# PSUM banks 4 to 7 as buffers of their own, keys loaded whole, values without regrouping, a re-planned order and zero matmuls, in a fused attention and feed-forward kernel on one core

## The chip, the core and the metric

The kernel runs on one core of a Trainium2 chip. The metric is the device time of one execution in microseconds (us), the median over runs. The profile is one execution recorded by the hardware profiler; its span runs from the first to the last instruction.

## The reference, cut to what matters

```python
batch, n_heads, seq, head_dim = (8, 8, 576, 64); n_pack = 32
def sm_attn(qq, kk, vv):                       # softmax(qq kk^T / 8) vv, per batch and head
    ...
p_packed = sm_attn(p, k, v)                    # 32 packed rows attend to 576 keys
out = sm_attn(q, p_packed, p_packed)           # 576 queries attend to the 32 packed rows
x = out.transpose(0, 2, 1, 3).reshape(4608, 512)
h = x @ w_in                                   # 512 -> 2048
g = np.maximum(h, 0.0) ** 2
return g @ w_out                               # 2048 -> 512
```

Inputs and output are float32; the kernel computes in bfloat16 with float32 accumulation.

## The kernel before, in words

**Work of one batch.** A batch has 8 heads, held as two groups ("qd") of four heads. Its steps carry short names, which the planner uses:

- Lk, Lq, Lv: loads of keys, queries and values, issued by POOL, which also turns them into bfloat16. Each key tile comes in two DMAs (L361, one for each half of a row's positions), each query tile in one (L357), the values of a batch in two (L366).
- Tk, Tq: 32x32 block transposes of the keys (L398) and queries (L393) on VectorE.
- G: a copy (L320 on VectorE) that regroups the loaded values v_b into v_g, so that two heads' 128 columns lie side by side.
- S1: scores of the packed rows, six matmuls (L409, L412); then the row maximum on VectorE (L416), the exponential on ACT (L420), the normalisation on VectorE (L426, L427). E: transposes of the result on TensorE (L433) and a copy out (tile e).
- PV: the packed values, ten matmuls for each qd, of 128 weight columns by 64 (L447). XT: eight small casts into the block-diagonal pq_bd and two casts into ppT.
- M: w_in times the packed values, four chunks of 512 columns, each chunk eight matmuls of 64x32 tiles (L474), then copies out to M. Because the second attention has only 32 packed rows, w_in is applied to these rows and not to all 576 queries.
- S2: scores of the queries (L495, L502); then maximum and subtraction (L514, L519), exponential on ACT (L525), sum, reciprocal and product on VectorE (L531, L532, L537). N: transposes of the result (L544, L547) and a copy out to a.
- F1: 16 steps of four matmuls (L560, M times a), each followed by a relu (L572 on ACT, L574 on VectorE) and a square (L582 on VectorE, L580 on ACT) into gT.
- F2: 36 output tiles of 128 tokens, each 16 matmuls of 512 columns (L590) that add up in one PSUM bank, then a copy to o_sb (L318 on ACT, L320 on VectorE) and four DMAs to the output. A batch is 4.5 such tiles.

**Order.** All engines work through their instructions in the order in which the program lists them. That order is made by a planner in the kernel (class Plan): it simulates the engines with assumed durations per step, takes at each moment the step with the best priority among the streams of steps (loads, transposes, first attention, M, second attention, F1, F2), and the instructions are then emitted in the order of the planned starts. TABLE holds an offset to each step's priority and a bias against ACT. HOP is the time assumed between a step's end and the start of what needs it. The loads stand in one stream: keys, values and queries of batch 0, w_in in 8 DMAs, half of w_out, batch 1 with the rest of w_out, then batches 2 to 7.

**PSUM.** Eight banks lie in four buffers of two banks each (`ps`). Banks 0 and 1, and 2 and 3, take S1, S2 and F1 (and, for some steps, F2); 4 and 5 take E, PV, N and the rest of S2; 6 and 7 take F2 tiles by turns. M takes banks 4 and 5 together with 0 and 1 or 2 and 3. What an instruction has to wait for is worked out by the framework from the buffers that it and earlier instructions touch.

**Slots.** 12 buffers hold key and query tiles, 4 hold values. POOL's loads take turns on eight DMA semaphores: a load waits until the load eight before it has landed.

`keep_clock` (a loop of matmuls of the zero tile with itself into the bank that is used next) exists before, but its count, `plan.fill`, stays 0 because `plan.warm` is 0.

Of the kernel before, what the change touches and what calls it, by code (L numbers as in the profile page):

```python
# [8 lines left out]
ACT = mybir.ActivationFunctionType  # L9
# [5 lines left out]
P = 128  # L15
# [9 lines left out]
HOP = 0.2  # L25
# [23 lines left out]
class Plan:  # L49
# [13 lines left out]
    def forward(self):  # L63
# [36 lines left out]
        while heap:  # L100
# [4 lines left out]
            while True:  # L105
# [40 lines left out]
                if e != "-":  # L146
                    busy[e] = f
                out.append(pc)
# [41 lines left out]
    def aim(self):  # L190
        for steps in self.streams:
            for st in steps:
                st.prio = self.prio.get(st.key, self.level(st))
                st.late = st.prio - (50.0 if st.key[:2] == "F2" else 0.25)
                st.lean = self.lean.get(st.key, 0.0)
# [6 lines left out]
    def run(self):  # L202
# [5 lines left out]
        for p in sorted(out, key=lambda p: p.start):  # L208
            e, us, fn = p.alts[p.alt]
            if e == "PE":  # L210
                self.fill = self.fills(p.start - free.get(e, 0.0), p.start)
# [15 lines left out]
TABLE = {'o': {'F1.1': -111.4, 'E.7': -15.38, 'F2.12': 29.55, 'F2.10': 62.36, 'PV.7': -8.82, 'Tk.5': -56.4, 'G.4':  # L227
    36.96, 'F2.32': 85.58, 'P.2': 78.86, 'G.2': 14.69, 'Tk.2': 14.82, 'Tq.2': 38.02, 'S1.2': -11.08, 'E.2': -36.13,
    'PV.2': 40.19, 'XT.2': 5.83, 'M.2': -3.06, 'S2.2': -26.61, 'C.2': -103.21, 'N.2': 47.99, 'F1.2': -28.89, 'C.5':
    -77.4, 'PV.4': -100.26, 'M.7': 3.35, 'G.3': -17.95, 'XT.0': 38.77, 'XT.1': 61.95, 'XT.3': -9.46, 'XT.4': -19.74,  # L230
    'XT.5': 39.77, 'XT.6': -76.62, 'XT.7': 28.4, 'F2.1': 28.92, 'P.0': 2.97, 'F2.24': 39.64, 'C.1': -16.13, 'C.3':
    -60.08, 'C.4': -34.32, 'C.6': -66.73, 'C.7': -8.09, 'X.0': 8.45, 'X.1': -10.2, 'I': -23.25, 'Tq.0': 5.27, 'Tq.3':
    67.76, 'G.5': 39.3, 'Tq.5': 26.97, 'S1.5': 3.18, 'E.5': -27.04, 'PV.5': 9.13, 'M.5': 25.95, 'S2.5': -32.33, 'N.5':
    60.11, 'F1.5': 20.76, 'F2.22': 41.33, 'E.4': -50.69, 'F2.4': 70.11, 'F1.0': 50.99, 'F1.3': 9.7, 'F1.4': -10.94,
    'F1.6': -33.13, 'F1.7': 61.34, 'S1.7': -26.63, 'Tk.3': 10.86, 'G.0': 18.04, 'Tk.0': 0.11, 'S1.0': -5.5, 'E.0':
    -43.01, 'PV.0': 24.59, 'M.0': 6.9, 'S2.0': -14.32, 'N.0': 3.07, 'F2.34': 79.86, 'F2.15': 128.64, 'Tk.4': -9.27,
    'Tq.4': -47.79, 'S1.4': -16.59, 'M.4': 25.83, 'S2.4': -4.33, 'N.4': -24.9, 'G.1': 11.86, 'G.6': 14.66, 'G.7':
# [632 lines left out]
```

## Time and profile before

| | |
|---|---|
| time, median of 3 runs | 310.99 us (308.6 to 311.1) |
| the profiled execution | 310.96 us, span 309.2 us |
| TensorE busy | 251.5 us (81%), 1920 matmuls |
| VectorE busy | 202.3 us (65%) |
| ACT busy | 163.8 us (53%) |
| POOL busy | 59.7 us (19%) |
| loads through POOL's queue | 18.60 MB in 33552 packets |
| chain that ended last | TensorE 65%, DMA 12%, ACT 9%, VectorE 8% |

How to read the lines below: a line of the timeline has the start (us from the span's start), the time taken, the engine (PE is TensorE, PEld its weight loads, DVE VectorE, SP the queue that issues the output DMAs), the line of the kernel, the operation, output<-input with shapes, a count, and in brackets how long the engine sat idle before it and what ended that. Ends of matmuls are modelled and include the passage through the pipeline. A line of the waits reads: who <- for whom: us in total, times, longest. The rows of the 40 slices give busy tenths of each engine; the DMA row is the busy share of the 16 DMA engines.

### The profile page before, as it was taken

What the parts mean: (1) busy time and instruction counts of PE and PEld (TensorE: products, weight loads), DVE (VectorE), ACT (ScalarE), POOL (GpSimd) and SP (SyncE); (2) the same over time, 40 slices, a digit from 0 to 9 for tenths busy, and PEclk for the clock granted to TensorE, in tenths of its full rate; (3) what the DMA queues carried; (4) which work ended last, traced back from release to release, by engine and by line L of the source; (5) the groups of instructions that cost most, each with busy time, mean ns of one, the idle gap of its engine ahead of it and who ended that gap; (6) DMA issues with size and microseconds to landing.
All of it is one profiled execution on the core that took longest, in us unless ns stands there. A gap on an engine that the chain in (4) does not pass through costs nothing.

```text
span 309.2 us, 5088 instructions
## 1 busy us (share of the span) xinstructions
PE 251.5 (81%) x1920; PEld 143.4 (46%) x1920; DVE 202.3 (65%) x370; ACT 163.8 (53%) x298; POOL 59.7 (19%) x91
## 2 busy tenths in 40 slices
PE   0244459769899899999999998899999898998883
PEld 0132326335555365555635564465655552465331
DVE  3667457888998856877997589765788456364000
ACT  3134346956734376666564766668876404274110
POOL 7559566530514010060000000000000000000000
PEclk9999999989999999999999999999999999999999
DMA  5999999998499861139321111111110121211222
GB/s 48 190 205 204 187 202 187 191 181 146 46 167 189 189 102 45 37 42 183 75 60 44 34 37 34 37 35 44 38 33 24 51 53 34 70 35 27 58 54 68
DMA packets 41016, 28.50 MB, mean 92 GB/s; under 512 B 17952, under 2 KB 34336, under 8 KB 40992
## 3 DMA queue, kind: packets, MB, share of 16 engines
q0 software_dynamic: 33552, 18.60, 41.5%
q1 hardware_dynamic: 6912, 9.45, 11.2%
q8 instruction: 15, 0.25, 0.4%
q10 hardware_dynamic: 528, 0.13, 0.2%
q14 instruction: 9, 0.07, 0.1%
HBM read 37.22 MB, written 9.44 MB: 151 GB/s over the span
## 4 chain that ended last, share of the span: by engine, by line
PE 65%; DMA 12%; ACT 9%; DVE 8%; issue 3%; POOL 1%; ACTq 0%; DVEq 0%; POOLq 0%
PE ps L590 38%; PE ps L560 17%; ACT o_sb L318 4%; DMA w_in_b<-in_moe_w_in_dram 3%; DMA q_b<-in_q_dram 3%; DMA w_out_b<-in_moe_w_out_dram 3%; DMA k_b<-in_k_dram 2%; ACT r L572 2%; PE ps L474 2%; PE ps L495 2%; PE ps L409 2%; DVE o_sb L320 1%; PE ps L544 1%; PE ps L433 1%; PE ps L447 1%
## 5 line engine op out<-in xcount | busy, mean ns | idle before, releaser
L590 PE MATMUL ps<-w_out_b,gT 128*128 128x512 bf16 x576 | 148.2, 380 | 15.0 <-ACT o_sb L318 11.8
L572 ACT ACTIVATE r<-ps 128x576 bf16<-128x576 f32 (+1 forms) x132 | 77.7, 611 | 41.7 <-PE ps L560 36.6
L560 PE MATMUL ps<-a,M 128*128 128x288 bf16 x512 | 83.4, 293 | 4.7 <-ACT r L572 1.7
L590 PEld LDWEIGHTS <-gT 128*128 128x128 bf16 x576 | 54.0, 98 | 62.8 <-issue 17.0
L560 PEld LDWEIGHTS <-M 128*128 128x128 bf16 x512 | 50.1, 100 | 39.7 <-issue 15.2
L582 DVE TENSOR_TENSOR gT<-r 128x576 bf16<-128x576 bf16 x121 | 51.6, 448 | 21.7 <-ACT r L572 20.7
L318 ACT COPY o_sb<-ps 128x512 f32<-128x512 f32 x27 | 15.8, 586 | 42.3 <-PE ps L590 38.3
L361 POOL DMA_DIRECT2D k_b<-in_k_dram x32 | 22.3, 703 | 38.8 <-DVE qT L393 22.7
L318 ACT CAST M<-ps 128x1024 bf16<-128x1024 f32 (+1 forms) x28 | 24.2, 896 | 10.4 <-PE ps L474 10.4
L398 DVE STREAM_TRANSPOSE kT<-k_b 128x1152 bf16<-128x1152 bf16 x16 | 21.5, 1361 | 9.5 <-DMA k_b<-in_k_dram 9.5
L409 PE MATMUL ps<-kT,pT_bd 128*128 128x256 bf16 x64 | 11.3, 307 | 14.8 <-DVE kT L398 14.6
L393 DVE STREAM_TRANSPOSE qT<-q_b 128x1152 bf16<-128x1152 bf16 x16 | 21.7, 1366 | 1.9 <-DMA q_b<-in_q_dram 1.9
L420 ACT ACTIVATE e1x<-ps,n 128x576 bf16<-128x576 f32 x16 | 11.9, 744 | 11.1 <-DVE n L416 8.3
L514 DVE TENSOR_REDUCE m<-ps 128x4 f32<-128x128 f32 (+2 forms) x17 | 11.8, 716 | 7.2 <-PE ps L495 4.3
L416 DVE TENSOR_REDUCE n<-ps 128x1 f32<-128x576 f32 x16 | 11.9, 745 | 5.7 <-PE ps L412 5.7
L474 PE MATMUL ps<-w_in_b,ppT 64*32 64x512 bf16 x256 | 11.2, 402 | 5.1 <-DVE d L519 2.1
L409 PEld LDWEIGHTS <-pT_bd 128*128 128x128 bf16 x64 | 6.3, 106 | 18.0 <-issue 9.6
L357 POOL DMA_DIRECT2D q_b<-in_q_dram x16 | 8.9, 560 | 25.4 <-DVE qT L393 18.7
L433 PE MATMUL ps<-ident,e1n 128*128 128x128 bf16 x80 | 8.2, 241 | 6.9 <-DVE e1n L427 6.6
L318 ACT COPY a<-ps 128x576 bf16<-128x576 bf16 x12 | 7.4, 640 | 11.7 <-PE ps L547 8.4
L525 ACT ACTIVATE e<-d 128x1152 bf16<-128x1152 f32 (+2 forms) x10 | 9.7, 969 | 6.4 <-DVE d L519 6.3
L531 DVE TENSOR_REDUCE t<-e 128x36 f32<-128x1152 bf16 (+2 forms) x10 | 11.0, 1103 | 2.3 <-ACT e L525 2.2
(54 smaller groups left out, 207.0 us busy)
## 6 DMA issues: line engine op xcount, KB each, us to landing
out_dram<-o_sb SPq DMA_DIRECT2D x144, 64.0 KB, 1.7
k_b<-in_k_dram POOLq DMA_DIRECT2D x32, 144.0 KB, 7.9
q_b<-in_q_dram POOLq DMA_DIRECT2D x16, 288.0 KB, 9.3
v_b<-in_v_dram POOLq DMA_DIRECT2D x8, 320.0 KB, 9.5
v_b<-in_v_dram POOLq DMA_DIRECT2D x8, 256.0 KB, 8.8
w_in_b<-in_moe_w_in_dram POOLq DMA_DIRECT2D x8, 256.0 KB, 10.2
w_out_b<-in_moe_w_out_dram POOLq DMA_DIRECT2D x8, 256.0 KB, 10.0
p_b<-in_p_dram POOLq DMA_DIRECT2D x1, 192.0 KB, 10.4
```

Source lines behind the costliest of these rows:

```text
L318: nc.scalar.copy(dst, src)
L361: nc.gpsimd.dma_start(t[:, j2 * VX * D:(j2 + 1) * VX * D], src[j2])
L393: nc.vector.transpose(self.qT[:, qd].rearrange("p dh (j a) -> p j dh a", a=32), self.t.q[qd][:].rearrange("p (j dh dl) -> p j dh dl", dh=2 ...
L398: nc.vector.transpose(kT[:, qd].rearrange("p dh (j a) -> p j dh a", a=32), self.t.k[qd][:].rearrange("p (j dh dl) -> p j dh dl", dh=2, dl=32))
L409: nc.tensor.matmul(main[:, i], lhsT=w[dh], rhs=kv[dh][:, i * GM:(i + 1) * GM], start=(dh == 0), stop=(dh == 1))
L416: nc.vector.tensor_reduce(self.n1[:, qd:qd + 1], self.ps1[qd], axis=AX.X, op=ALU.max, negate=True)
L420: nc.scalar.activation(e1x[:, qd], self.ps1[qd], ACT.Exp, bias=self.n1[:, qd:qd + 1], accum_out=self.d1[:, qd:qd + 1])
L474: nc.tensor.matmul(pair(u, j)[o:o + 32, qd, :], lhsT=self.ppT[64 * e:64 * e + 64, qd, pr, :], rhs=w_in_b[64 * e:64 * e + 64, qd * 2 + pr, ...
L560: nc.tensor.matmul(ps[:, c], lhsT=a.M[:, qd, fb * FB:(fb + 1) * FB], rhs=a.a2[:, qd, c * HALF:(c + 1) * HALF], start=(qd == 0), stop=(qd = ...
L572: nc.scalar.activation(dst, src, ACT.Relu)
L582: eng.tensor_tensor(out=Att.cols(gT[:, fb, o:o + S]), in0=r, in1=r, op=ALU.mult)
L590: nc.tensor.matmul(po[t], lhsT=gT[:, fb, n0:n0 + P], rhs=w_out_b[:, fb, :], start=(fb == 0), stop=(fb == NFB - 1))
```

## The change

- **PSUM.** Banks 0 to 3 stay as two buffers of two; banks 4 to 7 become four buffers of one bank each (`pb4` to `pb7`). M's second chunk of a pair is copied out of its two single banks by halves.
- **Keys.** One DMA loads a whole key tile, like a query tile. The positions then stand in another order along a row, and S1's matmuls write their scores with a stride of two columns, which restores the order that the values have.
- **Values.** v_g and its copies are gone; PV reads v_b as loaded. A weight tile is now one head's 64 columns, so PV has 20 matmuls of 64 weight columns by 32 for each qd instead of 10 of 128 by 64. The two heads of a pair land in the two halves of the partitions, so that ppT is one cast instead of two.
- **Slots.** 16 buffers for keys and queries, 5 for values.
- **Order.** A new TABLE, a new set of assumed durations, HOP 0.07 instead of 0.2 with 0.13 added after TensorE's steps, loads limited to eight under way in the plan and served in line. F2 tiles form two streams, the even and the odd ones. In the built order both N of batch 0 stand ahead of S1 of batch 1 (before: one of them after it); ahead of N of batch 1 stand 64 matmuls of F1 and 32 of F2 (before: 56 and 16). After the last F1 matmul 63 matmuls of F2 remain (before: 82).
- **Zero matmuls.** `plan.warm = 70.0`: where the plan has a gap of more than 0.45 us on TensorE within its first 70 us, matmuls of the zero tile (128x128 by 256 columns) are put in, one for each 0.115 us of the gap less 0.2. There are 160, in groups of 44, 6, 14, 4, 14, 11, 19, 11, 11, 4, 2, 13 and 7 in this order.

The numbers that TABLE holds are left out.

```diff
 INF = float("inf")
-HOP = 0.2
+HOP = 0.07
+LATE = {"PE": 0.13}
...
                 pc.start, pc.end, pc.alt = t, f, a
                 if e != "-":
                     busy[e] = f
+                f += LATE.get(e, 0.0)
                 out.append(pc)
...
             for st in steps:
                 st.prio = self.prio.get(st.key, self.level(st))
                 st.late = st.prio - (50.0 if st.key[:2] == "F2" else 0.25)
+                if st.key[0] == "L":
+                    st.late = -200.0 + 1e-3 * steps.index(st)
                 st.lean = self.lean.get(st.key, 0.0)
...
-            if e == "PE":
-                self.fill = self.fills(p.start - free.get(e, 0.0), p.start)
+            self.fill = self.fills(p.start - free.get(e, 0.0), p.start) if e == "PE" else 0
...
-    NKQ, NV = 12, 4
+    NKQ, NV = 16, 5
...
-        v_g = [consts.tile([P, GM + 1, H * D], BF16, name=f"v_g{i}") for i in range(2)]
         gT = consts.tile([P, NFB, 2 * S], BF16, name="gT")
-        ps = [psum.tile([P, 2, 512], F32, name=f"ps{i}") for i in range(4)]
+        ps = [psum.tile([P, 2, 512], F32, name=f"ps{i}") for i in range(2)]
+        ps += [psum.tile([P, 512], F32, name=f"pb{i}") for i in range(4, 8)]
...
         def keep_clock(t):
             for _ in range(plan.fill):
                 nc.tensor.matmul(t, lhsT=zero[:, :P], rhs=zero, start=True, stop=True)
             plan.fill = 0
 
+        def half(n):
+            return ps[n // 2][:, n % 2, :] if n < 4 else ps[n - 2][:]
+
         def bank(u, j=0):
-            t = ps[u[j] // 2][:, u[j] % 2, :]
+            t = half(u[j])
             keep_clock(t[:, :2 * P])
             return t
 
         def pair(u, j=0):
-            assert u[j] % 2 == 0 and u[j + 1] == u[j] + 1
+            assert u[j] in (0, 2) and u[j + 1] == u[j] + 1
             keep_clock(ps[u[j] // 2][:, 0, :2 * P])
             return ps[u[j] // 2]
...
-                self.v_raw, self.v = v_b[b % NV], v_g[b % 2]
+                self.v = v_b[b % NV]
 
             def dma_kq(self, name, qd):
                 t = getattr(self, name)[qd] = qkv.tile([P, JT * D], BF16, name=name + "_b", tag="kqb")
-                if name == "q":
-                    nc.gpsimd.dma_start(t, q[self.b, qd * QH:(qd + 1) * QH].rearrange("h (a j) d -> (h a) (j d)", j=JT))
-                else:
-                    src = k[self.b, qd * QH:(qd + 1) * QH].rearrange("h (j2 a x) d -> j2 h a (x d)", j2=2, x=VX)
-                    for j2 in range(2):
-                        nc.gpsimd.dma_start(t[:, j2 * VX * D:(j2 + 1) * VX * D], src[j2])
+                src = {"k": k, "q": q}[name]
+                nc.gpsimd.dma_start(t, src[self.b, qd * QH:(qd + 1) * QH].rearrange("h (a j) d -> (h a) (j d)", j=JT))
 
             def dma_v(self, i):
                 n = GM + i
                 src = v[self.b].rearrange("h (ap x) d -> ap h (x d)", x=VX)
-                nc.gpsimd.dma_start(self.v_raw[64 * i:64 * i + 64, :, :n * D], src[:, :, i * GM * D:(i * GM + n) * D])
-
-            def group(self, h0, h1, eng):
-                cast(eng, self.v[:, :, h0 * D:h1 * D].rearrange("p g (h d) -> p h g d", d=D),
-                     self.v_raw[:, h0:h1].rearrange("p h (g d) -> p h g d", d=D))
+                nc.gpsimd.dma_start(self.v[64 * i:64 * i + 64, :, :n * D], src[:, :, i * GM * D:(i * GM + n) * D])
...
                 ps = self.ps1[qd] = pair(u).rearrange("p c n -> p (c n)")[:, :S]
                 kv = [kT[:, qd, dh].rearrange("p (j2 x a) -> p x j2 a", j2=2, a=32) for dh in range(2)]
                 w = [pT_bd[:, self.b, qd, dh] for dh in range(2)]
-                main = ps[:, :GM * P].rearrange("p (g i n) -> p i g n", i=2, n=64)
+                main = ps[:, :GM * P].rearrange("p (g i a j2) -> p i g j2 a", i=2, a=32, j2=2)
+                rest = ps[:, GM * P:].rearrange("p (a j2) -> p j2 a", j2=2)
                 for i in range(2):
                     for dh in range(2):
                         nc.tensor.matmul(main[:, i], lhsT=w[dh], rhs=kv[dh][:, i * GM:(i + 1) * GM],
                                          start=(dh == 0), stop=(dh == 1))
                 for dh in range(2):
-                    nc.tensor.matmul(ps[:, GM * P:], lhsT=w[dh], rhs=kv[dh][:, 2 * GM], start=(dh == 0), stop=(dh == 1))
+                    nc.tensor.matmul(rest, lhsT=w[dh], rhs=kv[dh][:, 2 * GM], start=(dh == 0), stop=(dh == 1))
...
             def pv(self, qd, u):
                 if qd == 0:
-                    self.ps_pp = bank(u)
-                ps = self.ps_pp
+                    self.ps_pp = bank(u)[:, :P]
                 for pr in range(2):
-                    h0 = qd * QH + 2 * pr
-                    c0 = qd * P + pr * 64
+                    c0 = (2 * qd + pr) * NP
                     for g in range(GM + 1):
-                        nc.tensor.matmul(ps[:, c0:c0 + 64], lhsT=self.t.v[:, g, h0 * D:(h0 + 2) * D],
-                                         rhs=self.e1[:, qd, g, pr * 64:pr * 64 + 64], start=(g == 0), stop=(g == GM))
-
-            def extract(self, e, eng):
+                        for e in range(2):
+                            h = 2 * pr + e
+                            nc.tensor.matmul(self.ps_pp[64 * e:64 * e + 64, c0:c0 + NP],
+                                             lhsT=self.t.v[:, qd * QH + h, g * D:(g + 1) * D],
+                                             rhs=self.e1[:, qd, g, h * NP:(h + 1) * NP], start=(g == 0), stop=(g == GM))
+
+            def extract(self, eng):
                 self.tile_of("ppT", small, [P, NQD, 2, NP], BF16)
-                cast(eng, self.ppT[64 * e:64 * e + 64].rearrange("p qd pr i -> p (qd pr) i"),
-                     self.ps_pp[64 * e:64 * e + 64, :2 * P].rearrange("p (n i2 i) -> p n i2 i", i2=2, i=NP)[:, :, e])
+                cast(eng, self.ppT[:].rearrange("p qd pr i -> p (qd pr i)"), self.ps_pp)
...
             def m(self, c, u, j=0):
                 self.tile_of("M", mpool, [P, NQD, DFF], BF16)
+                keep_clock(half(u[j])[:, :2 * P])
                 for h in range(QH):
                     for qd in range(NQD):
                         pr, e = divmod(h, 2)
                         o = 32 * (h ^ qd)
-                        nc.tensor.matmul(pair(u, j)[o:o + 32, qd, :], lhsT=self.ppT[64 * e:64 * e + 64, qd, pr, :],
+                        nc.tensor.matmul(half(u[j + qd])[o:o + 32], lhsT=self.ppT[64 * e:64 * e + 64, qd, pr, :],
                                          rhs=w_in_b[64 * e:64 * e + 64, qd * 2 + pr, c * WCH:(c + 1) * WCH],
                                          start=True, stop=True)
-                self.psm[c] = pair(u, j)
+                self.psm[c] = u[j:j + 2]
 
             def m_out(self, c, eng):
-                cast(eng, self.M[:, :, c * WCH:(c + 1) * WCH], self.psm[c])
+                cast(eng, self.M[:, :, c * WCH:(c + 1) * WCH], ps[self.psm[c][0] // 2])
 
             def m_half(self, c, qd, eng):
-                cast(eng, self.M[:, qd, c * WCH:(c + 1) * WCH], self.psm[c][:, qd])
+                cast(eng, self.M[:, qd, c * WCH:(c + 1) * WCH], half(self.psm[c][qd]))
...
-        plan = Plan({"kqb": NKQ, "vb": NV, "r": 4, "osb": 3}, 8)
+        plan = Plan({"kqb": NKQ, "vb": NV, "r": 4, "osb": 3, "dq": 8}, 8)
...
-        def load_step(name, us, fn, slot=(), issue=0.62):
-            return Step(name, [[[("POOL", issue, fn)]], [[("DMA", us, lambda: None)]]], (), slot, (), lag=1.8)
+        def load_step(name, us, fn, slot=[], issue=0.56):
+            return Step(name, [[[("POOL", issue, fn)]], [[("DMA", us, lambda: None)]]], (), slot + [("dq", 1)], [("dq", 1, None)], lag=LAG)
...
         def pv_steps(b):
             nm = f"PV.{b}.0"
-            return [Step(nm, [[[("PE", 0.45, lambda: T[b].pv(0, U[nm]))]]],
-                         [f"E.{b}.0", f"G.{b}.0"], banks=AB),
-                    Step(f"PV.{b}.1", [[[("PE", 0.45, lambda: T[b].pv(1, U[nm]))]]],
-                         [f"E.{b}.1", f"G.{b}.1"]),
+            return [Step(nm, [[[("PE", 0.29, lambda: T[b].pv(0, U[nm]))]]],
+                         [f"E.{b}.0", f"Lv.{b}.0", f"Lv.{b}.1", "I2" if b else "I"], banks=AB),
+                    Step(f"PV.{b}.1", [[[("PE", 0.29, lambda: T[b].pv(1, U[nm]))]]],
...
                                        ("ACT", 0.82, lambda x=x: T[b].pq_block(x, A))] for x in range(2)]
-                                     + [[("DVE", 0.23, lambda e=e: T[b].extract(e, V)),
-                                         ("ACT", 0.24, lambda e=e: T[b].extract(e, A))] for e in range(2)]],
+                                     + [[("DVE", 0.27, lambda: T[b].extract(V)),
+                                         ("ACT", 0.28, lambda: T[b].extract(A))]]],
...
@@ -698,12 +684,14 @@
                 def mm(c=c, nm=nm):
                     T[b].m(c, U[nm], 0)
                     T[b].m(c + 1, U[nm], 2)
-                res.append(Step(nm, [[[("PE", 0.66, mm)]],
-                                     [[("ACT", 1.02, lambda x=x: T[b].m_out(x, A)),
-                                       ("DVE", 1.22, lambda x=x: T[b].m_out(x, V))] for x in (c, c + 1)]],
-                                [f"XT.{b}/1.{i}" for i in (2, 3)] + [f"LWI.{x}.{i}" for x in (c, c + 1) for i in range(2)]
+                res.append(Step(nm, [[[("PE", 0.56, mm)]],
+                                     [[("ACT", 1.02, lambda c=c: T[b].m_out(c, A)),
+                                       ("DVE", 1.22, lambda c=c: T[b].m_out(c, V))]]
+                                     + [[("ACT", 0.6, lambda c=c, x=x: T[b].m_half(c + 1, x, A)),
+                                         ("DVE", 0.7, lambda c=c, x=x: T[b].m_half(c + 1, x, V))] for x in QDS]],
+                                [f"XT.{b}/1.2"] + [f"LWI.{x}.{i}" for x in (c, c + 1) for i in range(2)]
                                 + ([f"F1.{b - 2}.{NFB - 1}"] if b > 1 else []),
-                                banks=[(4, 5) + x for x in HB], free=[(1, None)]))
+                                banks=[x + (4, 5) for x in HB], free=[(1, None)]))
...
+        LAG = 2.4
...
-        plan.base.update(DVE=3.0, POOL=0.8, ACT=0.8, SP=0.3, DMA=2.5, PE=3.6)
+        plan.base.update(DVE=2.4, POOL=1.2, ACT=2.1, SP=0.3, DMA=3.0, PE=3.0)
...
-        plan.stream(sum([g_steps(b) for b in range(B)], []))
...
         plan.stream(sum([f1_steps(b) for b in range(B)], []))
-        plan.stream(f2_steps(0))
-        plan.stream(f2_steps(1))
-        x, y = f2_steps(2, "F2.2.0", 0), f2_steps(3, "F2.2.0", 1)
-        plan.stream([z for i in range(NFB) for z in (x[i], y[i])])
-        plan.stream(sum([f2_steps(t) for t in range(4, NT)], []))
+        plan.stream(sum([f2_steps(t) for t in range(0, NT, 2)], []))
+        plan.stream(sum([f2_steps(t) for t in range(1, NT, 2)], []))
         plan.use(TABLE)
+        plan.warm = 70.0
```

## The prediction

> **What bounds the kernel now.** I read the page first (spans, the 40 slices, the chain), then the table by stage, then TensorE's waits after the start-up, then three stretches of the timeline.
>
> ```profile
> span 309.2 us, 5088 instructions
> PE 251.5 (81%) x1920; PEld 143.4 (46%) x1920; DVE 202.3 (65%) x370; ACT 163.8 (53%) x298; POOL 59.7 (19%) x91
> PE   0244459769899899999999998899999898998883
> DMA  5999999998499861139321111111110121211222
> ```
>
> ```profile
> 0.00:68.06 68.06, 33.32 (x281) 20.80 (x282) 44.07 (x84) 32.74 (x70) 43.36 (x66) 0.99 1.19 178
> 68.06:304.20 236.14, 218.19 (x1641) 122.58 (x1640) 158.23 (x286) 130.49 (x227) 16.32 (x25) 1.00 0.35 68
> ```
>
> The stage rows give the time in PE, PEld, DVE, ACT and POOL, then the granted clock, the DMA share and GB/s. I cut at 68.06 us, where the second batch's transposes (L544) end. Before the cut TensorE is busy 33 of 68 us and loads stream at 178 GB/s. After it TensorE idles 17.95 us of 236, and these waits explain nearly all of that:
>
> ```profile
> PE ps L590 <- ACT o_sb L318: 11.8, 20, 0.7
> PE ps L590 <- DVE o_sb L320: 3.2, 6, 0.8
> PE ps L560 <- ACT r L572: 1.1, 2, 0.7
> ```
>
> The tail shows what such a wait is:
>
> ```profile
> 287.83 3.61 PE L590 MATMUL ps<-w_out_b,gT 128*128 128x512 bf16 x16 [0.67 <-ACT o_sb L318]
> 291.48 0.58 ACT L318 COPY o_sb<-ps 128x512 f32<-128x512 f32 x1 [3.70 <-PE ps L590]
> 292.12 3.61 PE L590 MATMUL ps<-w_out_b,gT 128*128 128x512 bf16 x16 [0.67 <-ACT o_sb L318]
> ```
>
> One output tile takes 16 matmuls. The next tile goes to the other bank, yet it starts 0.06 us after the copy out of the previous bank ends (291.48 + 0.58 = 292.06). Banks 6 and 7 lie in one buffer, so the wait is for the buffer and not for data.
>
> In the start-up VectorE's in-order queue is what runs late:
>
> ```profile
> 40.13 0.83 DVE L320 COPY v_g<-v_b 128x2560 bf16<-128x2560 bf16 x1 [2.01 <-DMA v_b<-in_v_dram]
> 40.87 0.75 DVE L416 TENSOR_REDUCE n<-ps 128x1 f32<-128x576 f32 x1
> 43.98 1.38 DVE L393 STREAM_TRANSPOSE qT<-q_b 128x1152 bf16<-128x1152 bf16 x1 [1.89 <-DMA q_b<-in_q_dram]
> 53.39 1.05 PE L495 MATMUL ps<-pq_bd,qT 128*128 128x128 bf16 x16 [0.21 <-DVE r L574]
> 66.61 0.58 PE L544 MATMUL ps<-ident,n 128*128 128x128 bf16 x4 [0.25 <-ACT M L318]
> ```
>
> The row maximum of batch 1 (L416) sits behind a regrouping copy that waits for a load. The second attention's scores (L495) start at 53.39 though the last query transpose was done at 47.5. Its transposes (L544) wait for M's copy out of banks 4 and 5, again one buffer.
>
> **Work at full pace.** TensorE's price of each step is the distance to the next start in dense stretches. F2: (3.61 - 0.38)/15 = 0.2153 us per matmul. F1 (four matmuls): 281.46 to 281.95 = 0.49. S1 0.49 (140.97 to 141.46), E 0.28, PV 0.29 per half (146.27 to 146.56), S2 with its rest 1.22 (150.38 to 151.60), M 0.56 per 16 matmuls (156.43 to 156.99), N 0.45 (108.04 to 108.49). A batch's attention is 2x0.49 + 2x0.28 + 2x0.29 + 1.22 + 2x0.56 + 2x0.45 = 5.37, eight are 43.0. F1 is 128x0.49 = 62.7 and F2 576x0.2153 = 124.0. All: 229.7 us. By 68.06 before has issued 14 F1 steps, 16 F2 matmuls and two attentions: 6.86 + 3.44 + 10.74 = 21.0. So the start-up loses 47.0. From there to the last matmul's end (304.14) 208.7 us of work take 236.1: 27.4 lost. The tail is 309.2 - 304.14 = 5.06.
>
> **The change part by part.**
>
> *Single banks.* 26 waits go: 15.0 us idle, and each also exposes the pipeline's end, 0.38 - 0.2153 = 0.165, together 4.3. That is -19.3, and leaves 27.4 - 19.3 = 8.1. Late next is ACT's relu: where F1 and F2 alternate, two F1 steps cost TensorE 0.98 plus three F2 matmuls 0.65 = 1.63, and ACT two relus, 1.36. There is room, but little, so I add 3 of new waits. Nearest row: the F1 waits for ACT and VectorE (L560, 1.1) against the 15 that go. Bounds 0 and 10, half of what was removed.
>
> *No regrouping, keys whole.* VectorE loses seven copies of 0.818 and two of 0.502, 6.7 us, and 16 small ppT casts of about 0.28 become eight. None binds after the cut (158 busy of 236), so they count only through the start-up. POOL issues 73 - 16 = 57 DMAs. Sixteen key issues at 0.70 go; a whole tile's issue is taken from the query row, 0.56, so the first six loads are issued by about 4.9 us instead of 6.6. Around 32 to 35 us, where the half key loads stand in line, the rate fell from 205 to 164-178 GB/s; I give 1.5 us to the second query's landing, bounds 0 and 3. Values now wait only at PV, on TensorE: behind that stand F1 and F2, but the values of batch 1 land at about 40 and PV comes later. The waits that follow on the eight DMA semaphores now hold more bytes; 16 key/query and 5 value slots instead of 12 and 4 remove a wait of 22.7 us on POOL that nobody on the path felt.
>
> *PV by halves.* 20 matmuls of 64 columns by 32 replace 10 of 128 by 64. Before shows no such tile. Upper end: each pair at today's 29 ns, 0.58 per half, +0.29x16 = +4.6. Lower end: the 16 small weight loads of M took 0.14 us, 9 ns each, 0.18, so -1.8. I take +2, nearer today's pair because the load still feeds all 128 rows. The Trainium skill (TensorE: Matmul & The Clock Gate, "Wait — 56ns, not 53.3ns?") says that starts never come closer than about 25 ns however narrow the matmul, which speaks against the halves: 20 x 25 = 0.5 per half would make it +3.4, and no row here shows it for 32 columns.
>
> *Strided score writes (S1).* The 64 large matmuls write every second column. No row shows strided writes; the strided reads of the same matmuls run at 0.49 per six, so I take 0, at most double, 0.49x14 = +7 after the start-up. A gain is excluded, since as many columns pass.
>
> *Zero matmuls.* 160 are in the built order, 44 ahead of the first scores, 94 until the first N. They fill a slow start: the four matmuls of L409 take 1.01 us at 11.34 and 0.60 at 140.97, though the granted clock reads 1.00 in both rows.
>
> ```profile
> 11.34 1.01 PE L409 MATMUL ps<-kT,pT_bd 128*128 128x256 bf16 x4 [11.34 <-DVE kT L398]
> 140.97 0.60 PE L409 MATMUL ps<-kT,pT_bd 128*128 128x256 bf16 x4
> ```
>
> At the slow pace 44 x 0.215 = 9.5 us from about 1.1 end at 10.6, just when the keys are transposed (11.3 before). Gain on batch 0's chain if they work, from slow and fast rows of S1, E, PV, S2 and N: 0.41 + 0.27 + 0.29 + 0.93 + 0.3 = 2.2. Loss if the pace stays slow: 94 x 0.108 = 10 us in that chain. Both mostly vanish in batch 1's wait for its loads, which cover some 10 us here. The same page ("What you observe") has the pace double after some 4 us of sustained matmuls; by it the first group alone would suffice and the loss would be 0.
>
> *The order.* The built order puts both N of batch 0 ahead of batch 1's scores (before: one waits behind them, 32.4 and 36.9), both e1n ahead of the query transposes, and all 16 F1 steps and 32 F2 matmuls ahead of batch 1's N. Work issued there: 7.84 + 6.89 + 10.74 less half an M 0.56 = 24.9, against 21.0. When? The last query transpose ended at 47.5, now about 45.5; S2 follows (batch 1's pq casts, eight of 0.2 on ACT, end by 44). From S2's start 1.2, then VectorE and ACT 1.22+0.28+1.21+0.27+1.16+1.35+0.38+1.34 = 7.2, six hops of about 0.06, and 1.3 for a pT transpose and relus queued between: N at 55.6, done at 56.5; I take 57. Lower end 54.5 (nothing between). Upper end 64: S2 at 49 plus 13.2 as before, and 2 more.
>
> *Sum.* 57 + (229.7 - 24.9) + 8.1 + 3 + 2 + 5.06 = 280.0. The profiled execution took 310.96 for a span of 309.2, so 1.8 is added: 281.8, call it **282**. The median of the runs, 310.99, is the same as the profiled one.
>
> **The rivals.** A: as above, 282. B: the waits change their names. The bank wait hid relus and squares that are late anyway; half of the 19.3 comes back, 292. For it: ACT has 0.27 us of slack in 1.63. Against: in the stage after the cut ACT is busy 130 and VectorE 158 of 236. C: the start-up is bound by loads. If batch 1's N stays at 64 despite the order, 7 us are missing, 289; for it 178 GB/s through the cut, against it the 5.9 us between the last query transpose and S2. D, on the other side: the order is too tight. The planner's hop falls from 0.2 to 0.07 us; all queues are in order, and 289 groups of TensorE follow the second N. If each arrives x later than planned, 289x is lost; at x = 0.10 it is 29 and the gain is gone, at 0.13 (the whole reduction) 282 + 38 = 320. Against: copy to matmul took 0.06 in the rows above, and matmul to copy 0.04 after an end that includes 0.165 of pipeline, the 0.07 and 0.13 now assumed.
>
> **How the numbers follow.** A 0.62, B 0.18, C 0.13, D 0.07. A's own range is 270 to 290: low 54.5 + 204.8 + 4 (half of the other waits) - 1.8 + 5.1 + 1.8 = 268, cut to 270 because all low ends together are unlikely. The full range reaches 298: 64 + 204.8 + 8.1 + 6 + 4.6 + 3.5 (half the strided cost) + 5.1 + 1.8 = 298. A measurement tells about 1% from no change; faster needs below 308. A to C all lie there; half of D lies beyond 314: faster 0.93, same 0.02, slower 0.05.
>
> **What would show it.** Right: no L590 wait for o_sb in the tail and under 3 us in all; the last tiles 3.45 us apart; N of batch 1 near 57; early S1 at 0.60 per four; PV 0.3 to 0.6 per half; no v_g. Wrong: new waits of TensorE for r or gT of over 10 us (B); L495 of batch 1 after 50 (C); short waits at most group boundaries (D); the strided L406 at twice its time.

## The result and the profile after

The changed kernel takes 283.64 us (median of 4 runs, 282.2 to 284.84) against 310.77 us before (308.6 to 311.1): a ratio of 0.914, 95% interval 0.907 to 0.921. The four runs lie in two pairs, 282.2 and 282.5 us at a mean granted clock of 1.000 and 0.999, and 284.7 and 284.8 at 0.993 and 0.989; the profiled execution is the one of 282.2 us, with a span of 280.4. The page of the changed kernel:

```profile
span 280.4 us, 5691 instructions
PE 265.5 (95%) x2240; PEld 157.9 (56%) x2240; DVE 195.7 (70%) x349; ACT 162.2 (58%) x316; POOL 46.4 (17%) x76
PE   8976998899999999999999999999999999999992
DMA  7999999999999971011122012111112011211132
```

TensorE is busy from the first slice on, and the loads are done in slice 15. The row of busy time flatters, though: it counts the zero matmuls, and matmuls that run at half pace. The table by stage, cut where batch 1's N (L541, L544) ends, now at 58.41 us:

```profile
0.00:58.41 58.41, 49.39 (x488) 34.72 (x489) 42.15 (x78) 32.29 (x76) 35.17 (x57) 1.00 1.20 193
58.41:275.60 217.19, 216.13 (x1753) 123.20 (x1752) 153.58 (x272) 129.47 (x241) 11.27 (x19) 1.00 0.37 78
```

Behind the cut TensorE idles 1.06 of 217 us (before: 17.95 of 236). The largest of TensorE's waits, over the whole span:

```profile
PE pb L304 <- ACT M L322: 2.1, 3, 0.7
PE pb L304 <- DVE d L516: 2.1, 1, 2.1
PE ps L304 <- ACT r L569: 2.0, 2, 1.3
PE ps L304 <- DVE zero L327: 1.1, 1, 1.1
PE pb L587 <- ACT gT L577: 1.0, 1, 1.0
```

No F2 matmul (now L587) waits for a copy to o_sb. Four of the five lines belong to L304, the zero matmuls. The timeline of TensorE in the same kernel shows, in order of time, the start, one of those waits, one half of PV, one S1 and the end:

```profile
1.07 6.52 PE L304 MATMUL ps<-zero 128*128 128x256 bf16 x44 [1.07 <-DVE zero L327]
7.42 1.03 PE L406 MATMUL ps<-kT,pT_bd 128*128 128x256 bf16 x4
...
21.77 2.23 PE L304 MATMUL pb<-zero 128*128 128x256 bf16 x19 [2.08 <-DVE d L516]
23.93 0.41 PE L471 MATMUL pb<-w_in_b,ppT 64*32 64x512 bf16 x8
...
41.22 0.49 PE L444 MATMUL pb<-e,v_b 128*64 128x32 bf16 x20
41.65 0.39 PE L587 MATMUL pb<-w_out_b,gT 128*128 128x512 bf16 x1
...
85.12 1.03 PE L406 MATMUL ps<-kT,pT_bd 128*128 128x256 bf16 x4
85.94 0.32 PE L409 MATMUL ps<-kT,pT_bd 128*128 128x64 bf16 x2
86.06 1.49 PE L587 MATMUL pb<-w_out_b,gT 128*128 128x512 bf16 x6
...
261.61 13.76 PE L587 MATMUL pb<-w_out_b,gT 128*128 128x512 bf16 x63
```

The last 63 matmuls run without a break. S1 starts at 7.42 us (before 11.34), but its six matmuls take 86.06 - 85.12 = 0.94 us, where before they took 0.49. A half of PV takes 41.65 - 41.22 = 0.43 us instead of 0.29. And 19 zero matmuls wait 2.08 us for a bank that VectorE still reads, then run for 2.2 us ahead of the M matmuls that need the bank.

From 58.41 to the end of the last matmul, 261.61 + 13.76 = 275.37, 204.8 us of work (the prediction's prices) take 217.0: 12.2 are lost. Twelve of the 16 S1 and PV halves lie behind the cut, so S1 accounts for 12 x 0.45 = 5.4 and PV for 12 x 0.14 = 1.7; 5.1 remain.

### The profile page after: what moved, and what is told of

Read it like the earlier page. It is cut to its first block, busy times and chain, and to the rows that moved or that the text cites. A ratio compares the mean times of both kernels' runs of the same rounds, so it can differ in the third digit from the quotient of the medians.

```text
span 280.4 us, 5691 instructions
## 1 busy us (share of the span) xinstructions
PE 265.5 (95%) x2240; PEld 157.9 (56%) x2240; DVE 195.7 (70%) x349; ACT 162.2 (58%) x316; POOL 46.4 (17%) x76
## 4 chain that ended last, share of the span: by engine, by line
PE 88%; DVE 5%; ACT 5%; issue 1%; ACTq 0%; DVEq 0%
PE pb L587 43%; PE ps L557 21%; PE ps L406 5%; PE ps L304 4%; PE ps L492 3%; PE pb L304 2%; PE ps L471 2%; PE pb L444 2%; PE pb L541 2%; PE pb L471 1%; ACT r L569 1%; PE pb L430 1%; ACT M L322 1%; DVE qT L389 1%; DVE pq_bd L324 1%
## 5 line engine op out<-in xcount | busy, mean ns | idle before, releaser
L587 PE MATMUL pb<-w_out_b,gT 128*128 128x512 bf16 x576 | 144.2, 380 | 1.0 <-ACT gT L577 1.0
L587 PEld LDWEIGHTS <-gT 128*128 128x128 bf16 x576 | 54.1, 99 | 53.7 <-issue 4.2
L322 ACT COPY o_sb<-pb 128x512 f32<-128x512 f32 x27 | 15.8, 586 | 23.9 <-PE pb L587 23.8
L304 PEld LDWEIGHTS <-zero 128*128 128x128 bf16 x160 | 16.1, 103 | 11.1 <-issue 7.2
L389 DVE STREAM_TRANSPOSE qT<-q_b 128x1152 bf16<-128x1152 bf16 x16 | 21.5, 1361 | 0.0
L322 ACT CAST M<-pb 128x512 bf16<-128x512 f32 x26 | 14.6, 594 | 5.1 <-PE pb L471 5.1
L406 PE MATMUL ps<-kT,pT_bd 128*128 128x256 bf16 x64 | 16.4, 411 | 0.0
L322 ACT CAST M<-ps 128x1024 bf16<-128x1024 f32 x13 | 13.1, 1009 | 5.4 <-PE ps L471 5.3
L304 PE MATMUL ps<-zero 128*128 128x256 bf16 x90 | 12.6, 297 | 3.1 <-ACT r L569 2.0
L322 ACT CAST pq_bd<-pb 32x64 bf16<-32x64 f32 x52 | 10.5, 203 | 6.6 <-DVE pq_bd L324 4.4
L511 DVE TENSOR_REDUCE m<-ps 128x32 f32<-128x1024 f32 (+1 forms) x9 | 9.9, 1101 | 4.4 <-PE ps L492 4.2
L366 POOL DMA_DIRECT2D v_b<-in_v_dram x16 | 11.2, 707 | 9.8 <-DMA k_b<-in_k_dram 8.4
L304 PE MATMUL pb<-zero 128*128 128x256 bf16 x70 | 8.6, 273 | 4.2 <-ACT M L322 2.1
## 6 DMA issues: line engine op xcount, KB each, us to landing
q_b<-in_q_dram POOLq DMA_DIRECT2D x16, 288.0 KB, 10.9
```

Of the source, the lines that this page charges most:

```text
L304: nc.tensor.matmul(t, lhsT=zero[:, :P], rhs=zero, start=True, stop=True)
L322: nc.scalar.copy(dst, src)
L366: nc.gpsimd.dma_start(self.v[64 * i:64 * i + 64, :, :n * D], src[:, :, i * GM * D:(i * GM + n) * D])
L389: nc.vector.transpose(self.qT[:, qd].rearrange("p dh (j a) -> p j dh a", a=32), self.t.q[qd][:].rearrange("p (j dh dl) -> p j dh dl", dh=2 ...
L406: nc.tensor.matmul(main[:, i], lhsT=w[dh], rhs=kv[dh][:, i * GM:(i + 1) * GM], start=(dh == 0), stop=(dh == 1))
L587: nc.tensor.matmul(po[t], lhsT=gT[:, fb, n0:n0 + P], rhs=w_out_b[:, fb, :], start=(fb == 0), stop=(fb == NFB - 1))
```

## The experiments

Every kernel was timed in three rounds beside the kernel before. Lines keep the numbers of the kernel they come from, which an edit can shift by a few.

### Single banks alone, and all but them

```diff
-        ps = [psum.tile([P, 2, 512], F32, name=f"ps{i}") for i in range(4)]
+        ps = [psum.tile([P, 2, 512], F32, name=f"ps{i}") for i in range(3)]
+        ps += [psum.tile([P, 512], F32, name=f"pb{i}") for i in range(6, 8)]
```

This is the kernel before, with only banks 6 and 7 as buffers of their own.

> The kernel before, with one part of the change alone: banks 6 and 7 as two buffers; order and all else as before. Theory (the 26 waits of F2 for o_sb are waits for a shared buffer and cost 15.0 us of idle time and 4.3 of exposed pipeline): 310.8 - 19.3 = 291.5 us, between 288 and 295, and fewer than 3 us of L590 waits for o_sb left. Rival (the waits change their names: relus and squares that are late anyway take over half): about 301 us, with new waits of TensorE for r or gT of some 10 us.

Measured: 291.52 us (291.27 to 292.19), ratio 0.939 (0.936 to 0.943), which is 19.3 below the 310.79 beside it. The tail of its timeline:

```profile
266.78 17.86 PE L591 MATMUL pb<-w_out_b,gT 128*128 128x512 bf16 x81
```

81 F2 matmuls in a row; no wait for o_sb is left. Batch 1's N ends at 67.59 (before 68.06), and from there to 284.64 the 208.7 us of work take 217.1: 8.4 lost, where the prediction left 8.1.

The reverse edit joins banks 6 and 7 in the changed kernel:

```diff
-        ps += [psum.tile([P, 512], F32, name=f"pb{i}") for i in range(4, 8)]
+        ps += [psum.tile([P, 512], F32, name=f"pb{i}") for i in range(4, 6)]
+        ps += [psum.tile([P, 2, 512], F32, name="pb6")]
```

> The changed kernel with one part undone: banks 6 and 7 in one buffer again, 4 and 5 stay single, order as changed. Theory: nearly every one of the 36 output tiles begins while the copy of the one before is due, at up to 0.75 us each; 283.6 + 15 to 20 = 299 to 304 us, and the idle time shows at L587 behind o_sb. Rival (the new order with two streams of output tiles hides it): under 289 us.

Measured: 302.75 us (301.51 to 304.02), ratio 0.975 (0.970 to 0.980), 19.1 above the changed kernel. Its waits:

```profile
PE pb L588 <- ACT o_sb L323: 11.0, 16, 0.9
PE pb L588 <- DVE o_sb L325: 4.5, 7, 0.8
```

The waits are back, 15.5 us in 23 places. So 19 of the 27 us are the two banks, under either order.

### Zero matmuls: none, or into a bank that nobody uses

```diff
-        plan.warm = 70.0
+        plan.warm = 0.0
```

> The changed kernel without the 160 zero matmuls, order as changed. Theory (the start-up hangs on the landing of batch 1's queries, so the fills hardly count): the first S1 takes 1.5 times as long or more and batch 0's N come 2 to 4 us later, but batch 1's N ends within 2 us of 58.4; 283.6 to 286 us. Rival (the fills carry the start-up): batch 1's N ends after 62, 289 us or more. Third: fills stand in the way, and without them it is under 282.

Measured: 279.67 us (278.51 to 279.97), ratio 0.900 (0.897 to 0.903): 4.0 faster without them. Its timeline and its table by stage:

```profile
7.88 1.87 PE L406 MATMUL ps<-kT,pT_bd 128*128 128x256 bf16 x4 [7.88 <-DVE kT L394]
```

```profile
20.00:30.00 10.00, 5.64 (x46) 2.70 (x38) 7.02 (x18) 5.10 (x10) 9.09 (x13) 0.50 1.23 207
```

The start really is slow without them: the first S1 takes 1.87 us for four matmuls instead of 1.03, and the granted clock is 0.50 between 20 and 30 us. Yet batch 1's N ends at 56.13, 2.3 earlier than with them, which is also what the two profiled executions differ by (282.2 and 279.97 us). The zero matmuls bring pace and cost more than it gives.

The next kernel keeps them but writes them to bank 7, which has no other use before its first F2 tile, and only up to 27 us of the plan. The 134 ahead of batch 0's N stay, the 26 behind it go:

```diff
-                nc.tensor.matmul(t, lhsT=zero[:, :P], rhs=zero, start=True, stop=True)
+                nc.tensor.matmul(ps[5][:, :2 * P], lhsT=zero[:, :P], rhs=zero, start=True, stop=True)
...
-        plan.warm = 70.0
+        plan.warm = 27.0
```

> The changed kernel with its zero matmuls written to bank 7, which nothing uses before the first output tile, instead of to the bank that the next step uses; only the 134 ahead of batch 0's second N less the last four stay. Theory (the zeros cost 4 us because each group waits for the same bank as the step behind it and then runs in front of that step): the groups of 11, 19, 11 and 11 lose their waits of 0.7 to 2.1 us for M and d, batch 1's N ends at or before 56.1 as without zeros, 278 to 280 us. Rival 1 (the time of the zeros itself is too long for the gaps): no better than 283. Rival 2 (a full-pace start-up is worth something once the zeros don't stand in the way): under 277.5.

Measured: 277.47 us (277.24 to 278.01), ratio 0.893 (0.891 to 0.895), 6.2 below the changed kernel (4.2 between the profiled executions, 282.2 and 278.01) and 2.2 below the one without, at the edge of what the second rival had: full pace in the start-up is worth something. The same group as above in its timeline:

```profile
19.51 0.30 PE L499 MATMUL pb<-pq_bd,qT 128*64 128x128 bf16 x4
19.74 2.25 PE L304 MATMUL pb<-zero 128*128 128x256 bf16 x19
21.92 0.41 PE L471 MATMUL pb<-w_in_b,ppT 64*32 64x512 bf16 x8
```

The 19 now run inside the wait, and M starts as the bank comes free. Batch 1's N ends at 54.2, 4.2 earlier. Two things share this. In the changed kernel 13 of the 26 that are gone here ran ahead of S2 (45.48 to 46.89) and 7 ahead of an F1 step (52.72 to 53.48), together 2.2 us. The other 2.0 come from the 134 that still run. For these the work was not what cost time; it was that a group first waited for the bank of the next step and then ran in front of it.

### The stride of S1

The first kernel moves the stride from S1's writes to its reads; what the scores hold stays the same.

```diff
-                kv = [... .rearrange("p (j2 x a) -> p x j2 a", j2=2, a=32) ...]
+                kv = [... .rearrange("p (j2 x a) -> p x a j2", j2=2, a=32) ...]
-                main = ps[:, :GM * P].rearrange("p (g i a j2) -> p i g j2 a", i=2, a=32, j2=2)
+                main = ps[:, :GM * P].rearrange("p (g i a j2) -> p i g a j2", i=2, a=32, j2=2)
...
```

> The changed kernel with S1's columns in another order of work: the matmuls read the transposed keys with a stride and write their scores without one (the same result in the same places). Theory (the strided write is what doubles S1's pace from 0.49 to 0.94 us per six matmuls): S1 falls to about 0.49, 14 x 0.45 = 6.3 us are saved after the start-up, 277 us, between 275.5 and 279. Rival (single elements at a stride cost the same on the reading side): S1 stays at 0.9 or more, 283.6 us.

Measured: 285.3 us (283.95 to 286.75), ratio 0.919 (0.914 to 0.924), not to be told from the changed kernel. Its timeline, from one S1 to the next step:

```profile
87.87 1.13 PE L406 MATMUL ps<-kT,pT_bd 128*128 128x256 bf16 x4
88.84 0.29 PE L409 MATMUL ps<-kT,pT_bd 128*128 128x64 bf16 x2
88.97 1.46 PE L587 MATMUL pb<-w_out_b,gT 128*128 128x512 bf16 x6
```

1.10 us per six: reading every element from another place (neighbours lie 288 elements apart) costs no less than writing every second column, 0.94. The second kernel takes the stride off TensorE altogether. VectorE's key transposes, which touch every element anyway, write in the order of the scores, and S1 reads and writes in that order without a stride (its lines are left out):

```diff
-                    kT[:, qd].rearrange("p dh (j a) -> p j dh a", a=32),
-                    self.t.k[qd][:].rearrange("p (j dh dl) -> p j dh dl", dh=2, dl=32))
+                    kT[:, qd].rearrange("p dh (x a j2) -> p j2 x dh a", a=32, j2=2),
+                    self.t.k[qd][:].rearrange("p (j2 x dh dl) -> p j2 x dh dl", j2=2, dh=2, dl=32))
...
```

> The changed kernel (zeros and order as changed), but the block transposes of the keys on VectorE write them in the order of the scores, two columns apart, so that S1 reads and writes without a stride. Theory (a stride of two on either side of a matmul doubles its pace): S1 0.49 instead of 0.94, and 283.6 - 16 x 0.45 = 276.5 us if the transposes keep their 1.36 us, up to 279 if they take twice as long. Rival (the pace comes from something else in S1): S1 stays above 0.8, 283 us or more.

Measured: 276.97 us (276.2 to 278.17), ratio 0.891 (0.888 to 0.895), 6.7 below the changed kernel. Its timeline, and its groups on VectorE:

```profile
83.91 0.60 PE L406 MATMUL ps<-kT,pT_bd 128*128 128x256 bf16 x4
84.35 0.22 PE L409 MATMUL ps<-kT,pT_bd 128*128 128x64 bf16 x2
84.41 1.46 PE L587 MATMUL pb<-w_out_b,gT 128*128 128x512 bf16 x6
```

```profile
L394 DVE STREAM_TRANSPOSE kT<-k_b 128x1152 bf16<-128x1152 bf16 x16 | 22.9, 1454 | 1.0 <-DMA k_b<-in_k_dram 1.0
```

S1 is back at 0.50 us per six, and the transposes grew by only 1.454 - 1.364 = 0.09 us each: 1.4 us on an engine with time to spare against 6.7 on the one that sets the end.

### Whole keys against halves

```diff
+                    src = k[self.b, qd * QH:(qd + 1) * QH].rearrange("h (j2 a x) d -> j2 h a (x d)", j2=2, x=VX)
+                    for j2 in range(2):
+                        nc.gpsimd.dma_start(t[:, j2 * VX * D:(j2 + 1) * VX * D], src[j2])
...
-                main = ps[:, :GM * P].rearrange("p (g i a j2) -> p i g j2 a", i=2, a=32, j2=2)
+                main = ps[:, :GM * P].rearrange("p (g i n) -> p i g n", i=2, n=64)
...
```

The changed kernel with the two DMAs per key tile of before, and so S1 without a stride.

> The changed kernel with the keys loaded in two halves again, each with its own DMA, and S1 writing without a stride, as before; all else as changed. Theory: S1 back to 0.49 (-6.3 after the start-up), and the loads 0 to 3 us later in batch 1's queries: 277 to 281 us, so loading keys whole costs more than it brings. Rival (the halves cost the loads more, since they need more descriptors): 283.6 or more, with batch 1's N after 62.

Measured: 280.62 us (280.56 to 280.78), ratio 0.903 (0.901 to 0.905). Its first S1:

```profile
11.41 0.60 PE L410 MATMUL ps<-kT,pT_bd 128*128 128x256 bf16 x4 [3.19 <-DVE kT L398]
```

S1 starts at 11.41 and batch 1's N ends at 62.6, each some 4 later than with whole tiles. The load is the cause: VectorE's first key transposes wait for it in both kernels and start at 9.98 instead of 5.79. Undoing the keys is 3.0 faster than the change as built and 3.7 slower than whole keys with ordered transposes. Loading whole was right; the stride that it was bought with cost more.

### Both repairs together

```diff
-        plan.warm = 70.0
+        plan.warm = 0.0
...
+                    kT[:, qd].rearrange("p dh (x a j2) -> p j2 x dh a", a=32, j2=2),
```

> Both in one: no zero matmuls, and key transposes that write in the order of the scores. If the two gains add: 279.7 - 6.3 = 273.4 us, between 272 and 276. If part of S1's time was covered or the transposes take longer: 276 to 279.

Measured: 272.76 us (272.21 to 273.42), ratio 0.878 (0.875 to 0.881). The two gains, 4.0 and 6.7 alone, are 10.9 together: they add. With bank 7 in place of no zero matmuls:

> Two edits together: the zero matmuls go to bank 7, which nothing else uses before its first F2 tile, and only before 27 us of the plan; and VectorE writes the transposed keys in the order of the scores, so that S1 neither reads nor writes with a stride. Theory: the zero matmuls cost where they wait for a busy bank, and the stride costs in S1; the two lie in different places, so the gains add: 283.6 - 6.2 - 6.7 = 270.7 us, S1 0.50 per six, batch 1's N done by 55. Rival: batch 1's loads or VectorE's queue set its N, so that the gain of the earlier start is lost when VectorE's key transposes grow by 0.09 us each: 272.8 or more, as without zero matmuls.

Measured: 272.28 us (271.6 to 274.3), ratio 0.879 (0.874 to 0.883). This is the best median, but its interval covers that of the kernel without zero matmuls, so the two are not told apart. Its timeline at batch 1's S1:

```profile
32.39 0.61 PE L406 MATMUL ps<-kT,pT_bd 128*128 128x256 bf16 x4 [1.39 <-DVE kT L394]
```

Batch 0 is through early, and TensorE then waits 1.39 us for VectorE's key transposes, which wait themselves:

```profile
30.87 2.81 DVE L394 STREAM_TRANSPOSE kT<-k_b 128x1152 bf16<-128x1152 bf16 x2 [1.67 <-DMA k_b<-in_k_dram]
```

VectorE idles 1.67 us for the load of batch 1's keys. With bank 7 and the strided S1 it idles 1.19 and 0.32 us for the same loads, without zero matmuls not at all. So of the rival's two causes it is the loads; the 0.09 us by which each transpose grew are small beside them. N ends at 53.58, 0.9 earlier than without zero matmuls (54.5), where bank 7 brought 1.9 as long as S1 had its stride (54.2 against 56.13).

### The order

```diff
-HOP = 0.07
-LATE = {"PE": 0.13}
+HOP = 0.2
+LATE = {}
```

> The changed kernel planned with the old assumption of 0.2 us from a step's end to what needs it (and nothing added after TensorE's steps); all else as changed, so only the order of the instructions differs. Rival D of the prediction (the order is too tight, groups on TensorE arrive later than planned and the in-order queue pays): the looser order is faster, below 282. Theory: the tight order costs nothing, since TensorE idles 1.06 us of 217 after the start-up; the offsets of the table were found for the tight plan, so another plan is the same or a little slower, 283 to 290, with waits of TensorE that have names instead of none.

Measured: 289.15 us (288.79 to 289.57), ratio 0.931 (0.928 to 0.934), 5.5 above the changed kernel. Its table by stage:

```profile
0.00:61.62 61.62, 51.32 (x487) 35.26 (x490) 43.74 (x86) 32.11 (x70) 35.87 (x59) 1.00 1.19 194
61.62:282.20 220.58, 214.28 (x1721) 123.16 (x1752) 149.55 (x268) 133.88 (x242) 10.46 (x18) 1.00 0.35 74
```

With the same work ahead of it, batch 1's N is 3.2 later, and what follows takes 3.4 more, in short waits of F1, F2 and M for r and gT. The looser plan is slower at both ends: the tight one was not too tight, though this run can't say how much of the 5.5 is the assumption itself and how much a table that was made for another one.

The old TABLE (its entries for G left out) in the changed kernel:

> The changed kernel with the priorities of the kernel before (those of the dropped regrouping steps left out), so single banks, keys loaded whole and zero matmuls stay and only the order goes back towards the old one. Theory: the order brought the part of the gain that is not the F2 banks (283.6 + 19 = 302.7 with joined banks, 291.5 before with single banks): batch 1's N is later than 58.4 with less work ahead of it, and TensorE waits for r and M after it: 288 to 296 us, batch 1's N done at 60 to 68. Rival: the single banks alone make any order good, the order brings nothing of its own: 282 to 286 us.

Measured: 289.54 us (289.19 to 290.04), ratio 0.932 (0.929 to 0.935), 5.9 above the changed kernel. Batch 1's N ends at 68.06, with about 4.9 us more work ahead of it. Its timeline there:

```profile
22.79 3.63 PE L306 MATMUL pb<-zero 128*128 128x256 bf16 x19 [2.08 <-DVE d L518]
...
56.80 1.80 PE L306 MATMUL ps<-zero 128*128 128x256 bf16 x15 [1.77 <-ACT r L571]
...
60.36 1.80 PE L306 MATMUL ps<-zero 128*128 128x256 bf16 x15 [0.67 <-DVE M L326]
```

Part of this is again zero matmuls that wait and then hold up M (2 x 1.8), and 1.4 us are the 19 that ran slower here (3.63 against 2.23). So the order has worth, but the table's own part is below 5.9, and this table too was made for another plan.

### The values

The kernel keeps the changed order's table and brings back v_g, PV with 128 weight columns and two ppT casts, with 15 key and query slots and 4 of values:

```diff
+            def group(self, h0, h1, eng):
+                cast(eng, self.v[:, :, h0 * D:h1 * D].rearrange("p g (h d) -> p h g d", d=D), ...)
...
-                        for e in range(2):
-                            ...
+                        nc.tensor.matmul(ps[:, c0:c0 + 64], lhsT=self.t.v[:, g, h0 * D:(h0 + 2) * D], ...)
```

> The changed kernel with the values regrouped as before: v_g and its copies on VectorE, PV of ten matmuls of 128 weight columns by 64, two casts to ppT (15 key and query slots and 4 of values, since the regrouped tiles need their space). Theory: PV goes back from 0.43 to 0.29 us per half, 14 x 0.14 = 2.0 us less on TensorE after the start-up; the copies, 6.7 us on VectorE, are hidden there; before it they delay batch 1 by 0 to 3: 281.5 to 285 us. Rival: VectorE's in-order queue is what sets the start-up, a copy that waits for a load holds what stands behind it: 286 us or more, with batch 1's N after 61.

Measured: 282.46 us (281.49 to 284.39), ratio 0.910 (0.906 to 0.914), not to be told from the changed kernel. Batch 1's N ends at 59.49, 1.1 later, and the half of PV is back at 0.29:

```profile
69.33 0.45 PE L449 MATMUL pb<-e,v_g 128*128 128x64 bf16 x10
69.62 1.15 PE L563 MATMUL ps<-a,M 128*128 128x288 bf16 x8
```

Dropping the copies paid nothing: N is 1.1 earlier without them, and the twelve halves of PV behind it cost 12 x 0.14 = 1.7 more on TensorE.

## Why the prediction held, step by step

282 was forecast and 283.6 measured, inside both ranges. The total held better than its parts. The prediction counts 14 S1 halves after the start-up; the traces have 12 behind batch 1's N, before and after.

- **Single banks, -19.3: held.** 19.3 measured when done alone, 19.1 when undone alone. The arithmetic, visible wait plus 0.165 us of exposed pipeline for each, was right to a few tenths; the 15.0 of idle time alone would have missed a fifth.
- **"Leaves 8.1", plus 3 of new waits: the first held, the second did not come.** With the banks alone 8.4 were left. In the changed kernel 5.1 remain beside S1 and PV, instead of 11.1. The room of 0.27 us that ACT has in each pair of F1 steps was enough, and rival B (292) is out: waits of F1 and F2 for r and gT are far below 10 us.
- **PV by halves, +2: held.** 0.14 x 12 = 1.7 behind the cut, 2.2 for all 16. The Trainium skill (TensorE: Matmul & The Clock Gate, "Wait — 56ns, not 53.3ns?") has a floor of about 25 ns between starts, from which the prediction estimated 3.4 for all 16; here 20 starts take 0.43 us, 21.5 ns each.
- **Strided score writes: "I take 0, at most double" failed as a value, and held as a bound.** 0.94 instead of 0.49 per six, 5.4 us after the start-up, where double the time would be 12 x 0.49 = 5.9. Twice the time of L406 was named as a sign of being wrong, and it came nearly so (1.03 against 0.60). The wrong turn was to take the row of strided reads as the nearest: those reads stay contiguous over 32 columns, and the kernel with reads that do not took 1.10. The Trainium skill (SBUF — State Buffer, "Door 1: The DMA port swizzle (why `[64,N]` ≈ `[32,N]`)") says that any non-contiguous access to PSUM slows matmuls considerably; the rows here agree. That rule spoke against the change and was not weighed.
- **"Early S1 at 0.60 per four" as the sign of the pace: failed.** It took 1.03 at 7.42 and 1.03 at 85.12. The pace was full; the stride alone made the duration look slow: with ordered transposes the first four, behind the same zero matmuls, take 0.60.
- **Zero matmuls, "Both mostly vanish in batch 1's wait for its loads": failed.** There is no such wait in the changed kernel. The transposes of batch 1's queries start at 42.01 with no wait for a DMA, right behind the steps of its first attention, which follow batch 0's N. What is gained or lost there arrives at the end: bank 7 brings N 4.2 us earlier, and the two profiled executions differ by 4.2. The pace itself came as hoped: the first 44 took 6.35 us to the next start, against the 9.5 of the slow pace. The possible loss was looked for in the pace and was in the bank: keep_clock writes to the bank of the next step, as the front of this document says, and the prediction did not follow that to its wait. (Ahead of batch 0's N the trace has 134 of them, 90 behind the first scores; the prediction counted 94.)
- **Keys whole, 1.5 us: mis-sized.** About 4 at the start, seen at S1 and at N alike. The sum had put the gain on the second query's landing and none on the first key.
- **No regrouping, hidden: held for the total.** 282.46 with it, though N is 1.1 later.
- **The order, N at 57: held closely**, 58.41. The last query transpose ended at 44.64 (forecast 45.5), and 13 zero matmuls stood ahead of S2 from 45.48 to 46.89. Rival C (loads set the start) is out for the changed kernel, and shows only where the zero matmuls go to bank 7 and batch 0 is through earlier. Rival D is out too: the group boundaries show no short waits, and the looser plan is slower.

So errors of opposite sign met: S1's 5.4 us taken as 0 and an N 1.4 later, against 6 us of other losses (11.1 forecast, 5.1 found) that did not come. That the sum of 280.0 came within 0.5 us of the span of 280.4 is in part luck. How the 18.8 us between the kernel with the banks alone (291.5) and the one with both repairs (272.8) divide among whole keys, banks 4 and 5, slots, and the planner's settings other than TABLE and HOP was not tried.

## What to carry to other kernels

If an engine waits for the copy out of another bank than the one it writes, look at what the buffer covers, and price each such wait as its idle time plus the exposed pipeline. If a layout must be turned somewhere, let the engine do it that touches every element anyway and has time to spare, not the reads or writes of the matmuls that set the end. Work that is to fill a gap must depend on nothing that ends the gap: check which buffer it writes before counting it as free.

## What was not expected of the hardware

The pace can be lost again after a single wait. In the kernel with key halves, S1 runs at full pace after an idle of 3.19 us (0.60 per four, 11.41), and the next, at 12.92, takes 1.01. The same instructions do not always fare alike: the wait of 2.08 us for d was passed at full pace in the changed kernel (19 zero matmuls in 2.23 us) and in three others. In the kernel with banks 6 and 7 joined the same 19 after the same wait took 3.29, with strided reads 3.84, with the old TABLE 3.63. In the first of these the granted clock was 0.83 between 20 and 30 us:

```profile
20.00:30.00 10.00, 6.61 (x58) 4.30 (x57) 4.91 (x13) 3.11 (x7) 9.69 (x13) 0.83 1.22 207
```

What decides it is not shown. The first group varies too: its 44 zero matmuls took 6.52 us in the changed kernel and 7.89 with banks 6 and 7 joined, where the first S1 so begins at 8.80 instead of 7.42. In the changed kernel's trace neither loss is seen.

The record of the clock does not tell all: in the kernel with both repairs and no zero matmuls it reads 1.00 from 0 to 20 us, and yet the first S1 takes 1.01 us for four matmuls, where 0.60 is the full pace. Its F1 matmuls at 26.56 take 2.28 us for eight, with a record of 1.00 between 20 and 30 us; without the ordered transposes the same eight take the same 2.28 at 28.02, with a record of 0.50.
